# A fused attention, convolution and gated feed-forward kernel: the first feed-forward product split into three float16 products, the last batch in three query groups, a new order

## The chip, the cores and the metric

The kernel runs on one core of a Trainium2 chip. Its engines work side by side, each through its own list of instructions in order: TensorE (PE, with PEld for its weight loads), VectorE (DVE), ScalarE (ACT), GpSimd (POOL), and SyncE (SP), which issues every DMA here. They meet through semaphores. The metric is the device time of one execution in microseconds (us), lower is better. A profile gives the span from the first instruction to the last, which lies about 2 us under the time of the same execution.

## The reference

```python
def _attn_ref(q, k, v):                    # q, k, v: 4 batches x 8 heads x 1152 x 64, float32
    q_pool = q.reshape(B, H, S // 2, 2, D).mean(axis=3)          # 576 queries a head
    scores = (1 / np.sqrt(D)) * np.matmul(q_pool, k.transpose(0, 1, 3, 2))
    scores = scores - np.max(scores, axis=-1, keepdims=True)
    attn = np.exp(scores)
    attn = attn / (np.sum(attn, axis=-1, keepdims=True) + 1e-09)
    return np.matmul(attn, v)

def _moe_ref(x, w_in, conv_w, w_out):      # x: 4 x 576 x 512 (the heads side by side)
    h = np.maximum(x @ w_in, 0.0)          # 512 -> 1024, the "first product"
    hp = np.concatenate([zeros, h, zeros], axis=1)               # one token of padding at each end
    conv_out = sum(conv_w[k] * hp[:, k:k + S, :] for k in range(3))
    gate = 1.0 / (1.0 + np.exp(-conv_out))
    return h * gate @ w_out                # 1024 -> 512, the "second product"
```

The weights arrive as float64 words and are turned into float32 on the chip by bit operations (`weights`).

## The kernel before

Heads are worked in 16 pairs, four pairs to a batch. For each pair `loads` brings q, k and v, and brings v into float16 high and low parts, scaled by a power of two that is found from the largest sum of absolute values of a row (`abs_v`, `spread_v`, `top_v`, `pow_v`, `scale_v`, `hi_v`, `lo_v`).

`softmax(o, d)` handles one block of 128 queries of each head (d = 0 to 3; d = 4 holds the last 64 of both heads). PE makes the scores in float32 (L404), DVE takes the maximum of each row (L416), ACT the exponential with its sum (L421), DVE the inverse of the sum in two small instructions (L433, L437). For most heads the normalized block is written as a float16 high part (L460 on ACT or L455 on POOL) and a low part (DVE, L463), and both are transposed by DMA (L476). For the seven heads of `X32` it stays float32: it is normalized (L493) and PE transposes it (L506, taken out of PSUM at L511).

`values(o, y)` is the product with v for a query group y: 256 queries (d = 0, 1) or 320 (d = 2, 3, 4). It takes three float16 matmuls for each of nine blocks of keys (L535; for the `X32` heads one float32 matmul, L541). The two heads of a pair fill the two halves of the array's columns. ACT writes the result as float32 into `x` (L548).

`feed(b, u)` makes the first product for 255 or 321 tokens of a batch: for each of eight slices of 128 hidden columns four float32 matmuls over 257 or 323 columns (L575), which the trace shows as two passes each, so eight records in all. ACT applies the relu (L581); ACT or POOL makes the first tap (L585, L589), DVE the other two (L596), ACT the tanh (L602), DVE the gate (L606). `second(b, t)` makes the second product for one block of 128 tokens (L639; 64 tokens at t = 4, L645), ACT takes it out (L653), SP stores it.

The order of all work is fixed beforehand: every step is a task, the table ORDER says in which order the tasks are emitted, SLOTS which buffer of its ring each takes, and SWAPPED which tasks run on their other engine. Each engine runs its own tasks strictly in that order. For example a pair's low part is the task

```python
t = add("DVE", dve(S) - 0.025, low, after=[t], uses=[ps_[e], sm, hl], port=True)
```

The text below calls one block S: the second product of batch 2 for its tokens 256 to 383 (t = 2), eight matmuls of L639. It is the place from which the work left is PE's above all.

Of the kernel before, what the change touches and what calls it, by code (L numbers as in the profile page):

```python
# [8 lines left out]
F32 = mybir.dt.float32  # L9
# [54 lines left out]
class Plan:  # L64
# [23 lines left out]
def unpack(words):  # L88
# [29 lines left out]
pcCrpUCZpdpVpXqCCLp4p2Cspyp5qgCpqECIpYCMqdCJCtCSp6CKp7CBBXpZqeC0CNpiqaCuqhCCC1pWCvqbqip8qfCOqqqcpjCPCTC2qJqSCU
qrCQqKCVqsp9DdqLC3CWCwqjqtqnDkqTCXqoDequqyqMDfqNCDqUCYqvqpqkDgqVqODlqlqPq5qxC4qWDyqzqmqRqXqQC6rYq6qwCRq7tcqYq8
rWDzC7DrqZq9q2q0DFDmuADhDAC5raq3DGDsDnDtq4DBriC8C9DCrvDoDDq1DiDuqArbrwrfrjrxtdrZDaDprcDErgrlr1DHrdrhDbqBrmrkr2  # L120
DIDcrnreDqDvryDwroDjrpr3DxrIDLDJrqrsDZrzDMrrDNrJtfrKDOrttgrLDPrArurBr4rFDQuvrCD0rDrMsarGDRrEsdsbD1seDKDSr5rQsf
rNscr6rOr7rPD2sgqIshskrRsnsitir0sqsosjDTslspDUsrrHr9sssAuxD3sDstsmsBsxDVsEsCsyDWr8sFsNtethDXsGsQsHsOrSsusIszsK
sRsLsSDYEpsvsPsMtjsTtsrTs0sJttEqsXtks1tuEbtlswsYtvEcEduyEeEiErtwsUtxEfEDsVEgEjEss2EwsWtyEhtCs3tmEttFtnEEtDEkuu
ExtIsZEFs4tGEyEREltHEmuzEzD5tJESETD6tztos5s8tAtKs6tps7D7s9EuEntSEvtBtqEKtTtLtUtEEAtVtrELEGtPt5EMtWEBE5uwtMEHD4
EovNtQEID8EUE6ENtXEJEYD9tYE7EVEOuKt6tZEZE0EPEWtaEQt2tNECt7tOE8E1t3FcuBuLt4t0uMt8tbEXE9t1FduiE2t9FeuCvPFquDuauE
tRE3ubFaFfFjucFgFbFrudvQFxFhuFFsuGFkufFlFmFEFyujueugukuXFzFiFtFFuhuNulFnumFLuOunuPvMFSE4upFAFMuQFuuUuouYuRuqFN
uZuSFOvauTuruVFGuHu0FPvbFZuWu1vcF0FBu2uIuJFQvdFoFHvOFCFpvRvAFIu3FJveu4FvF1u7u5FTF2u8vfusFUvgu9vBvkF3FRvCFVFwF4
vlvnvTFWvmFKvqutFDFXFYvUF6GdvhvVvou6F5vrGevDvsviF7vEvpvjv5vFv2vWEaGfv3vHvtv6vxF8vuv7vGF9vyGav4vzv8wivXv9vvwfGb
wavwwcvIwgwjwhwdwswbwkvJwvwlwmGjwevYwnvZGkwtwpGcGlwov0wwGgwqwxwuv1GmwrGhwywzwFGnwAwIwCGovKwGwJwHwDwKw0wBwLwMwP
wEwSwNvSw1vLGvwTwUwOGJGwwVGxwWHbGKwXGXHcwQwYGyGCwZGYGLGMwRGQGDGEGFGzGpGAGZGqG0G1GNGrGOGPGsGBGRGSG4GtGTGuGUGGw2  # L130
G5Hiw3GHG2GVGWHpHjG6HkHdHeG3HwHfHqG7HgGIHrHhHlHmHKHxHsHtG8G9HYHLHyHMHzHaHAHRHBHZHCHDHSHTHUH0HNHnHVH5HoHWH1HuHX
HEHOIcH6H7HFH8H2IjHvH3HGIdIeHHHPIkIfHIH9IgIaHQIhIlIbH4IiHJImIqIpIxInIoIyIrIsIzIAItIBICGiIDIuIEIvIwIFIGIJIHIIIK
ILIMINIO
"""
SLOTS = (
    "00000010100011001001012110001020112111230321101030000011110011101011102001011120021102131022100031000201031111"
    "01112000002210221000012103110010000210201033011101011022210010001113011300100000110201101301110200013022101012"
    "03100111100000410100023011001110010101210223201013001011110231100200111521010121101111210020001320103200101112"
    "11101003101100000600002112200103011130021003221110013032210200111011120113100002112101011320303112121203111000"
    "02021002011100110112303211021302001031022000001113001120112011013002211010100031011122013011032000112000000111"  # L140
    "10112012100013012200231103011101123010001141210011222000201131031100123112003110100110000600112002203203110100"
    "12102331000123001010120011511112112302213200101010033211121112032301000001021020011002102112301002031102012211"
    "31301100110100002110032010121203011013312200121010000131200232210201012001311031232012103111204030001112001140"
    "10310204021100111101001001213011231304010210011020321411100100001110020140011033000203041001201042100312010110"
    "01010300211111431300110411211000221302140101111001"
)
SWAPPED = """
aeaobmb0dCeAeHfugcgqgGgZhjhxh5iiisiEiSjtjTkdkqkTk0lblLl8mbmimDm3ndnqntn5n8omoUo8pnqPrXsksxsUsXtftZuxuHuRu4vhvk
vuvxvEvZwmwpwMwPxcxlxVyNyWzezwzzz1AfAtAAAOCeCGCUC8ErEyEMETFeFlFNGxGEHdHkHFHTH7
"""  # L150

# [4 lines left out]
def tile_pooled_attention_conv_gate_ffn(  # L156
# [38 lines left out]
    wi = const.tile([P, KC, DFF], F32, name="wi")  # L195
    wo = const.tile([P, FC, DM], F32, name="wo")

# [4 lines left out]
    r_kt = Ring("kt", 3, sb, [P, S], F32)  # L202
    r_qt = Ring("qt", 2, sb, [P, K0], F32)
    r_qd = Ring("qd", 2, sb, [P, K1], F32)
    r_v = Ring("v", 2, sb, [P, 2, NC, P], F16)
# [4 lines left out]
    r_vs = Ring("vs", 3, sb, [P, 8], F32)  # L210
    r_x = Ring("x", 7, sb, [P, 578], F32)
    r_h = Ring("h", 5, sb, [P, 324], F32)
    r_g = Ring("g", 4, sb, [P, 4, 322], F32)
    r_o = Ring("o", 2, sb, [P, DM], F32)

    def pe(cycles):
        return cycles / 2400.0 + 0.1
# [6 lines left out]

    def gp(n):
        return 0.3 + n / 850.0


# [5 lines left out]
    for pr in range(NPAIR):  # L234
        o = Pair()
        o.pr, o.vin, o.qin = pr, Buf(r_vin), Buf(r_qin)
        o.kt, o.qt, o.qd = Buf(r_kt), Buf(r_qt), Buf(r_qd)

        o.x32 = [(pr, e) in X32 for e in range(2)]
        o.v, o.vs = Buf(r_v), Buf(r_vs)  # L240
        o.x = Buf(r_x)
        pairs.append(o)

    def loads(o):
# [54 lines left out]
        def abs_v():  # L299
            nc.scalar.activation(  # L300
                out=o.v[:, es].rearrange("p e c d -> p (e c d)")[:, 0:HS * len(two)],
                in_=o.vin[:, es].rearrange("p e c d -> p (e c d)"), func=AF.Abs, accum_out=o.vs[:, 0:1],
            )

        def spread_v():
            nc.tensor.matmul(
                out=wv[:, 0:P], lhsT=o.vs[:, 0:1].to_broadcast([P, P]), rhs=ident, start=True, stop=True
            )
# [530 lines left out]
```

## Time and profile before

| | |
|---|---|
| time, median of 3 runs | 652.01 us (650.74 to 653.11) |
| the profiled execution | 651.47 us, span 649.5 us |
| busy share of the span | PE 94%, DVE 82%, ACT 70%, POOL 24% |
| 16 DMA engines, hardware queue | 81.9% |
| granted TensorE clock, mean | 0.992 of 2.4 GHz |

A busy share is a mean over the whole span; stages differ, and a PE that counts as busy need not stream without a break. So the stages are read one by one from a table of windows, and what ended last is read from the chain of waits.

### The profile page before, as it was taken

How to read it: one execution, taken by the hardware profiler on the slowest of the kernel's cores; microseconds unless marked ns; L12 is line 12 of the kernel's file. 1: busy time of each engine (PE TensorE's matmuls, PEld its weight loads, DVE VectorE, ACT ScalarE, POOL GpSimd, SP SyncE). 2: the span in 40 equal slices, each digit the busy share in tenths (PEclk: the TensorE clock that was granted, in tenths of full speed). 3: DMA queues.
4: the chain of work that ended last, by engine and by line, in shares of the span. 5: the costliest groups of instructions: out<-in, count | busy, mean ns of one | idle time of the engine just before them, and what ended most of it. 6: DMA issues, size and time to landing. Idle time of an engine off the chain costs nothing. (4 is left out here: it accounts for less than half of the span.)

```text
span 649.5 us, 10435 instructions
## 1 busy us (share of the span) xinstructions
PE 612.6 (94%) x3805; PEld 380.1 (59%) x3805; DVE 535.5 (82%) x811; ACT 453.0 (70%) x775; POOL 158.7 (24%) x183
## 2 busy tenths in 40 slices
PE   4679898999999999999999999999999999999997
PEld 2355555666666655555666666455666655486643
DVE  4998999998899999788978899878988998764610
ACT  4998988787888776746678788757767765643410
POOL 0553334323231222221365000021231122220000
PEclk9998989899999999999999999999999999999999
DMA  8779988879875887999889998999998988983001
GB/s 279 190 207 196 215 227 168 187 150 228 178 179 122 171 201 139 229 203 209 167 221 179 233 154 204 197 180 215 191 220 167 172 191 162 192 134 58 0 22 67
DMA packets 279122, 113.72 MB, mean 175 GB/s; under 512 B 265376, under 2 KB 265888, under 8 KB 279072
## 3 DMA queue, kind: packets, MB, share of 16 engines
q1 hardware_dynamic: 279072, 113.07, 81.9%
q8 instruction: 30, 0.49, 0.3%
q14 instruction: 20, 0.16, 0.1%
HBM read 37.77 MB, written 4.72 MB: 65 GB/s over the span
## 5 line engine op out<-in xcount | busy, mean ns | idle before, releaser
L421 ACT ACTIVATE p<-s,sm 128x1152 f32<-128x1152 f32 x144 | 175.4, 1219 | 91.5 <-DVE sm L416 59.0
L416 DVE TENSOR_REDUCE sm<-s 128x1 f32<-128x1152 f32 x144 | 192.3, 1349 | 10.0 <-PE s L404 9.3
L404 PE MATMUL s<-kt,qt 64*128 64x512 f32 (+3 forms) x704 | 183.2, 471 | 17.2 <-ACT p L421 8.7
L463 DVE SCALAR_TENSOR_TENSOR hl<-p,sm,hl 128x1152 f16<-128x1152 f32 (+1 forms) x116 | 168.8, 1464 | 18.8 <-ACT hl L460 10.6
L404 PEld LDWEIGHTS s<-kt,qt 64*128 64x128 f32 (+1 forms) x704 | 89.1, 175 | 119.0 <-issue 81.9
L404 PE MATMUL s<-kt,qd 64*128 64x512 f32 x256 | 144.0, 647 | 0.0
L575 PE MATMUL a<-x,wi 128*128 128x257 f32 (+1 forms) x512 | 134.8, 414 | 0.6 <-ACT h L581 0.5
L535 PE MATMUL a<-pt,v 128*64 128x256 f16 (+1 forms) x1350 | 118.1, 288 | 0.1
L639 PE MATMUL a<-wo,g 128*128 128x512 f32 x256 | 115.1, 599 | 0.0
L575 PEld LDWEIGHTS a<-x,wi 128*128 128x128 f32 x512 | 93.8, 189 | 30.9 <-ACT h L581 1.9
L460 ACT ACTIVATE hl<-p,sm 128x1152 f16<-128x1152 f32 (+1 forms) x78 | 97.0, 1252 | 13.0 <-issue 3.9
L535 PEld LDWEIGHTS <-v 128*64 128x64 f16 x1350 | 87.8, 110 | 12.6 <-issue 4.4
L455 POOL TENSOR_SCALAR hl<-p,sm 128x1152 f16<-128x1152 f32 (+1 forms) x38 | 51.0, 1344 | 140.3 <-DVE sm L437 93.9
L639 PEld LDWEIGHTS a<-wo,g 128*128 128x128 f32 x256 | 47.1, 190 | 53.5 <-issue 51.4
L596 DVE SCALAR_TENSOR_TENSOR g<-h,cw,g 128x321 f32<-128x321 f32 (+1 forms) x128 | 65.1, 526 | 12.4 <-POOL g L589 8.5
L541 PE MATMUL a<-pt,v 128*64 128x256 f32 (+1 forms) x252 | 64.1, 409 | 0.5 <-ACT pt L511 0.5
L506 PE MATMUL a<-ident,p 128*128 128x128 f32 (+1 forms) x315 | 49.5, 280 | 14.0 <-ACT pt L511 6.4
L493 POOL TENSOR_SCALAR p<-p,sm 128x1152 f32<-128x1152 f32 (+1 forms) x27 | 37.6, 1394 | 87.6 <-DVE sm L437 68.4
L511 ACT ACTIVATE pt<-a 128x384 f32<-128x384 f32 (+2 forms) x98 | 45.0, 476 | 11.2 <-PE a L506 10.6
L506 PEld LDWEIGHTS a<-ident,p 128*128 128x128 f32 (+1 forms) x315 | 33.1, 143 | 27.6 <-ACT pt L511 8.9
L589 POOL TENSOR_SCALAR g<-h,cw 128x255 f32<-128x255 f32 (+1 forms) x24 | 17.4, 727 | 103.2 <-ACT h L581 92.8
L541 PEld LDWEIGHTS a<-pt,v 128*64 128x64 f32 x252 | 33.4, 137 | 11.1 <-ACT pt L511 1.0
(58 smaller groups left out, 467.6 us busy)
## 6 DMA issues: line engine op xcount, KB each, us to landing
qin<-in_q_dram SPq DMA_DIRECT2D x16, 640.0 KB, 5.2
kt<-in_k_dram SPq DMA_DIRECT2D x16, 576.0 KB, 4.9
vin<-in_v_dram SPq DMA_DIRECT2D x9, 576.0 KB, 4.7
g<-in_moe_w_in_dram SPq DMA_DIRECT2D x8, 512.0 KB, 5.0
qd<-qt SPq DMA_DIRECT2D x32, 128.0 KB, 4.1
g<-in_moe_w_out_dram SPq DMA_DIRECT2D x8, 512.0 KB, 4.3
out_dram<-o SPq DMA_DIRECT2D x16, 256.0 KB, 2.5
vin<-in_v_dram SPq DMA_DIRECT2D x7, 288.0 KB, 3.7
```

What stands on the lines that cost most here:

```text
L404: nc.tensor.matmul(out=w, lhsT=f, rhs=kk, start=True, stop=True)
L416: nc.vector.tensor_reduce(out=sm[:, e:e + 1], in_=runs(st[e]), axis=AX.XY, op=ALU.max, negate=True)
L421: nc.scalar.activation(out=p.tile().rearrange("p (a n) -> p a n", a=2), in_=runs(st[e]), func=AF.Exp, bias=sm[:, e:e + 1], scale=1.0, accu ...
L455: eng.tensor_scalar(out=hl[rows, 0], in0=ps_[e][rows], scalar1=sm[rows, 6 + e:7 + e], scalar2=1.0, op0=ALU.mult, op1=ALU.mult,)
L460: nc.scalar.activation(out=hl[rows, 0], in_=ps_[e][rows], func=AF.Copy, scale=sm[rows, 6 + e:7 + e])
L463: nc.vector.scalar_tensor_tensor(out=hl[rows, 1], in0=ps_[e][rows], scalar=sm[rows, 6 + e:7 + e], in1=hl[rows, 0], op0=ALU.mult, op1=ALU.s ...
L506: nc.tensor.transpose(w[:, (i - a1) * nq:(i - a1 + 1) * nq], ps_[e][rows, i * P:(i + 1) * P], ident[rows, rows])
L535: nc.tensor.matmul(out=to, lhsT=o.v[:, e, c, vc:vc + D], rhs=o.pt[y, e][:, hl * NC + c, 0:n], start=(c == 0 and j == 0), stop=(c == NC - 1 ...
L541: nc.tensor.matmul(out=to, lhsT=o.v[:, e, c].bitcast(F32), rhs=p32.rearrange("p (a n) -> p a n", a=NC)[:, c, 0:n], start=(c == 0), stop=(c ...
L575: nc.tensor.matmul(out=w[:, 0:n], lhsT=wi[:, j, f * P:(f + 1) * P], rhs=x.x[:, 255 * u:255 * u + n], start=(j == 0), stop=(j == KC - 1),)
L596: nc.vector.scalar_tensor_tensor(out=c, in0=h[:, t:t + tok], scalar=cw[:, f, t:t + 1], in1=c, op0=ALU.mult, op1=ALU.add)
L639: nc.tensor.matmul(out=w.tile(), lhsT=g[f // 4][:, f % 4, c:c + P], rhs=wo[:, f, :], start=(f == 0), stop=(f == FC - 1),)
```

## The change

Three things change together.

The first product is computed as three float16 matmuls in place of one float32 matmul (high times high, high times low, low times high). For that `w_in` is converted into the buffer of `w_out`, its row sums of absolute values are taken, and it is split into `wi` high and low (`split`); `w_out` is converted afterwards. The result of `values` goes to a new float32 buffer `xf`, and from there into `x` high (ACT or POOL) and `x` low (DVE). The scale of x for a batch comes from the v scales of its four pairs (`scales`), so the v scale is now found for the float32 heads too (`abs_one`, `most_v`). The relu undoes the scales.

The last batch has three query groups of 256, 256 and 64 queries, in `values` and `feed` alike (255, 256 and 65 tokens), and its pairs are worked interleaved, which the order table decides.

The order, the buffers and the engines of single tasks are searched anew, with one more buffer each for k, q and v. The small sum of the softmax (`total`) can run on ACT, normalizing a float32 head too, and the scaling steps of v move from POOL to DVE.

```diff
+GROUPS = [((0, 1), (2, 3, 4))] * 3 + [((0, 1), (2, 3), (4,))]
...
-    wi = const.tile([P, KC, DFF], F32, name="wi")
+    wi = const.tile([P, 2, KC, DFF], F16, name="wi")
...
-    r_kt = Ring("kt", 3, sb, [P, S], F32)
+    r_kt = Ring("kt", 4, sb, [P, S], F32)
...
-    r_x = Ring("x", 7, sb, [P, 578], F32)
+    r_xf = Ring("xf", 5, sb, [P, 320], F32)
+    r_x = Ring("x", 7, sb, [P, 2, 578], F16)
...
+        def abs_one():
+            m = HS * len(one)
+            nc.scalar.activation(
+                out=o.x.tile().rearrange("p a n -> p (a n)")[:, 1:1 + m] if m == HS else o.x[:, :, 1:1 + HS],
+                in_=o.v[:, of].bitcast(F32).rearrange("p e c d -> p e (c d)"), func=AF.Abs,
+                accum_out=o.vs[:, 6:7],
+            )
...
         def scale_v():
-            nc.gpsimd.tensor_scalar(
+            nc.vector.tensor_scalar(
...
-        iv = add("DVE", 0.265, inverse, after=ex, uses=[sm], port=True)
-        y = int(d > 1)
...
+        t = add("DVE", 0.13, total, after=ex, uses=[sm], port=True, alt=("ACT", 0.2, False))
+        iv = add("DVE", 0.135, inverse, after=[t], uses=[sm])
+        y = next(i for i, ds in enumerate(o.groups) if d in ds)
...
+        def high(eng):
+            if eng is nc.scalar:
+                nc.scalar.activation(out=o.x[:, 0, to], in_=xf[:, 0:n], func=AF.Copy, scale=o.bs[:, 2:3])
+                return
...
+        def low():
+            nc.vector.scalar_tensor_tensor(
+                out=o.x[:, 1, to], in0=xf[:, 0:n], scalar=o.bs[:, 2:3], in1=o.x[:, 0, to],
+                op0=ALU.mult, op1=ALU.subtract,
+            )
...
             def mm(f=f, w=w):
-                for j, x in enumerate(xs):
-                    nc.tensor.matmul(
-                        out=w[:, 0:n], lhsT=wi[:, j, f * P:(f + 1) * P], rhs=x.x[:, 255 * u:255 * u + n],
-                        start=(j == 0), stop=(j == KC - 1),
-                    )
+                for i, (a, c) in enumerate(((0, 0), (0, 1), (1, 0))):
+                    for j, x in enumerate(xs):
+                        nc.tensor.matmul(
+                            out=w[:, 0:n], lhsT=wi[:, a, j, f * P:(f + 1) * P], rhs=x.x[:, c, s0:s0 + n],
+                            start=(i == 0 and j == 0), stop=(i == 2 and j == KC - 1),
+                        )
...
             def relu(w=w, h=h):
-                nc.scalar.activation(out=h[:, 0:n], in_=w[:, 0:n], func=AF.Relu)
+                nc.scalar.activation(out=h[:, 0:n], in_=w[:, 0:n], func=AF.Relu, scale=xs[0].bs[:, 3:4])
...
+            def total():
+                _, lo32, hi32, mm, a = parts()
+                i = KC * c + j
+                nc.scalar.activation(out=mm, in_=a, func=AF.Abs, accum_out=ws[:, i:i + 1])
...
+                def low(src=src, to=to):
+                    nc.vector.scalar_tensor_tensor(
+                        out=wi[:, 1, to[0], to[1]], in0=src, scalar=ws[:, 12:13], in1=wi[:, 0, to[0], to[1]],
+                        op0=ALU.mult, op1=ALU.subtract,
+                    )
```

What the new order does is shown at three places by the instruction lists of single engines (name of the tile written, arrow, tiles read; `x3` counts equal neighbours). The first is DVE where the first feed-forward block begins, before (`g` holds the taps, the rows with `g<-g 128x512` and `wo` convert weights):

```order
L463 SCALAR_TENSOR_TENSOR hl<-p,sm,hl 64x1152
L705 TENSOR_SCALAR g<-g 128x512
L416 TENSOR_REDUCE sm<-s 128x1
L596 SCALAR_TENSOR_TENSOR g<-h,cw,g 128x255
L714 TENSOR_SCALAR wo<-g 128x512
L596 SCALAR_TENSOR_TENSOR g<-h,cw,g 128x255 x2
```

And DVE at the same place of the changed kernel:

```order
L609 SCALAR_TENSOR_TENSOR x<-xf,bs,x 128x320
L501 SCALAR_TENSOR_TENSOR hl<-p,sm,hl 128x1152
L446 TENSOR_REDUCE sm<-s 128x1
L609 SCALAR_TENSOR_TENSOR x<-xf,bs,x 128x320
L474 RECIPROCAL sm<-sm 128x2
L322 TENSOR_SCALAR vs<-vs 128x1
L446 TENSOR_REDUCE sm<-s 128x1
L501 SCALAR_TENSOR_TENSOR hl<-p,sm,hl 128x1152
L799 TENSOR_SCALAR g<-g 128x512
L689 SCALAR_TENSOR_TENSOR g<-h,cw,g 128x255
```

New there are the low parts of x (L609) between the softmax steps, while the sum before a reciprocal (L433 before) is gone from some places. In all, 239 DVE instructions stand ahead of the first tap, 243 before.

The second place is ACT at the start of the program, before:

```order
L421 ACTIVATE p,sm<-s,sm 128x1152 x2
L460 ACTIVATE hl<-p,sm 128x1152
L300 ACTIVATE v,vs<-vin 128x576
L421 ACTIVATE p,sm<-s,sm 128x1152
L701 ACTIVATE g<-g 128x512
L511 ACTIVATE pt<-a 128x3x128
```

And changed (L851 takes the absolute sums of `w_in`, L464 is the softmax's `total`, L532 normalizes a float32 head):

```order
L451 ACTIVATE p,sm<-s,sm 128x1152
L851 ACTIVATE g,ws<-wo 128x512
L451 ACTIVATE p,sm<-s,sm 128x1152
L289 ACTIVATE qt<-qin 128x640
L498 ACTIVATE hl<-p,sm 128x1152
...
L464 ACTIVATE sm<-sm 128x2
L451 ACTIVATE p,sm<-s,sm 128x1152
L532 ACTIVATE p<-p,sm 128x1152
```

ACT has taken in work between the exponentials: 196 instructions stand ahead of its first relu, 157 before.

The third place is the end of PE's list, before:

```order
L535 MATMUL a<-pt,v 64x320
L575 MATMUL a<-x,wi 128x257 x4
L575 MATMUL a<-x,wi 128x323 x32
L639 MATMUL a<-wo,g 128x512 x32
L645 MATMUL a<-wo,g 64x256 x16
```

And changed:

```order
L733 MATMUL a<-wo,g 128x512 x4
L668 LDWEIGHTS wi
L668 MATMUL a<-x,wi 128x67
...
L733 MATMUL a<-wo,g 128x512 x18
L739 MATMUL a<-wo,g_6567 64x256 x8
L739 MATMUL a<-wo,g_6628 64x256 x8
```

Before, all five blocks of the last second product stood behind the last first product; now 14 of the 32 matmuls of the four large blocks stand between the short 67-column groups.

## Rows read from the trace of the kernel before

**Rows 1.** The page, part 1: busy us (share of the span), instructions

```profile
PE 612.6 (94%) x3805; PEld 380.1 (59%) x3805; DVE 535.5 (82%) x811; ACT 453.0 (70%) x775; POOL 158.7 (24%) x183
```

**Rows 2.** Table of windows: stretch, length, busy us by engine (instructions), clock, DMA share

```profile
core 0: us, PE busy (x) PEld busy (x) DVE busy (x) ACT busy (x) POOL busy (x), PEclk, DMA share, GB/s
8.00:139.00 131.00, 111.62 (x751) 69.07 (x752) 121.99 (x191) 112.15 (x192) 48.54 (x47) 0.96 0.86 205
139.00:248.00 109.00, 106.79 (x696) 71.28 (x695) 102.33 (x162) 86.17 (x159) 30.43 (x38) 1.00 0.81 179
248.00:533.00 285.00, 282.52 (x1784) 172.76 (x1783) 250.10 (x364) 207.83 (x341) 62.31 (x72) 1.00 0.96 191
533.00:649.50 116.50, 111.59 (x582) 66.87 (x580) 59.33 (x93) 44.19 (x82) 16.71 (x22) 1.00 0.47 95
```

**Rows 3.** Timeline of PE where block S begins: start, us, instruction

```profile
532.95 1.02 PE L639 MATMUL a<-wo,g 128*128 128x512 f32 x2
```

**Rows 4.** Waits of DVE from 8 to 248: us in total, times, longest

```profile
DVE sm L433 <- ACT p L421: 4.7, 7, 1.4
DVE sm L416 <- PE s L404: 3.5, 8, 0.7
```

**Rows 5.** Pieces of the chain that ended last: start us, us, what, records

```profile
566.70 6.74 PE a L535 x108
...
574.66 8.88 PE a L575 x40
...
591.17 3.79 PE a L535 x54
594.96 19.37 PE a L575 x72
```

**Rows 6.** Timeline of PE, transposes of 64 columns after a load of 128

```profile
110.93 0.28 PE L506 MATMUL a<-ident,p 64*128 64x64 f32 x2
...
111.05 0.60 PE L506 MATMUL a<-ident,p 64*128 64x64 f32 x7
```

**Rows 7.** Groups of DVE by shape: busy us, mean ns, idle before

```profile
L463 DVE SCALAR_TENSOR_TENSOR hl<-p,sm,hl 128x1152 f16<-128x1152 f32 x109 | 157.9, 1456 | 18.6 <-ACT hl L460 10.6 <-POOL hl L455 6.1 <-POOL x L358 1.4
...
L596 DVE SCALAR_TENSOR_TENSOR g<-h,cw,g 128x321 f32<-128x321 f32 x64 | 34.4, 553 | 7.2 <-POOL g L589 5.5 <-ACT g L585 1.3
L596 DVE SCALAR_TENSOR_TENSOR g<-h,cw,g 128x255 f32<-128x255 f32 x64 | 31.1, 499 | 5.2 <-POOL g L589 3.0 <-ACT g L585 1.9
...
L352 DVE SCALAR_TENSOR_TENSOR v<-vin,vs,v 128x576 f16<-128x576 f32 x25 | 20.8, 846 | 2.4 <-POOL v L344 2.0 <-POOL x L358 0.4
...
L278 DVE TENSOR_TENSOR qin<-qin 128x640 f32<-128x640 f32 x9 | 7.4, 817 | 3.5 <-DMA qin<-in_q_dram 3.5
...
L493 DVE TENSOR_SCALAR p<-p,sm 128x1152 f32<-128x1152 f32 x7 | 5.7, 815 | 0.0
```

**Rows 8.** Pieces of DVE in the same chain: start us, us, what

```profile
547.30 0.17 DVE sm L433
...
547.58 0.06 DVE vs L321
...
584.57 0.89 DVE g L596 x2
```

**Rows 9.** Groups of ACT by shape: busy us, mean ns, idle before

```profile
L460 ACT ACTIVATE hl<-p,sm 128x1152 f16<-128x1152 f32 x73 | 90.8, 1252 | 11.6 <-ACT p L421 3.1 <-DVE sm L437 3.0 <-issue 2.6
...
L421 ACT ACTIVATION_READ_ACCUMULATOR p<-s,sm 128x1 f32 x144 | 28.3, 197 | 0.0
...
L548 ACT ACTIVATE x<-a,vs 128x256 f32<-128x256 f32 x16 | 7.5, 468 | 4.8 <-POOL x L358 3.1 <-PE a L535 1.5 <-PE a L541 0.2
```

**Rows 10.** Windows of the same table, two dense stretches

```profile
20.00:120.00 100.00, 84.03 (x574) 52.02 (x574) 94.59 (x154) 89.01 (x152) 39.03 (x39) 0.95 0.87 200
180.00:260.00 80.00, 78.72 (x467) 49.54 (x463) 76.79 (x116) 62.06 (x111) 19.26 (x25) 1.00 0.76 158
```

**Rows 11.** Timeline of PE where the first product begins

```profile
139.36 1.35 PE L575 MATMUL a<-x,wi 128*128 128x257 f32 x5
```

More of the change, by code (lines that the diff above doesn't have):

```diff
@@ L525, in values @@
     def values(o, y):
-        n = (256, 320)[y]
+        first = P * o.groups[y][0]
+        n = min(P * (o.groups[y][-1] + 1), HS) - first
         w = Buf(r_a)
@@ L545, in part @@
                             )
+        xf = Buf(r_xf)
+        to = slice(1 + first, 1 + first + n)
         def keep():
             nc.scalar.activation(
-                out=o.x[:, 1 + 256 * y:1 + 256 * y + n], in_=w[:, 0:n], func=AF.Copy,
-                scale=1.0 if all(o.x32) else o.vs[:, 4:5],
-            )
-        t = None
-        for i in range(1):
-            t = add("PE", (n * 27.0 / 2400 * (4 / 3 if any(o.x32) else 1) + 0.08), lambda i=i: part(i), mode=2,
-                    after=o.turned[y] + o.vls + ([t] if t else []),
-                    uses=[o.v, o.pt[y, 0], o.pt[y, 1]] + ([w] if i else []), takes=[] if i else [w])
@@ new lines, in low @@
+        def low():
+            nc.vector.scalar_tensor_tensor(
+                out=o.x[:, 1, to], in0=xf[:, 0:n], scalar=o.bs[:, 2:3], in1=o.x[:, 0, to],
+                op0=ALU.mult, op1=ALU.subtract,
+            )
+        t = add("PE", (max(n, 90) * 27.0 / 2400 * (4 / 3 if any(o.x32) else 1) + 0.08), lambda: part(0), mode=2,
+                after=o.turned[y] + o.vls, uses=[o.v, o.pt[y, 0], o.pt[y, 1]], takes=[w])
+        t = add("ACT", act(n, 0.1), keep, after=[t] + o.one, uses=[w] + ([] if all(o.x32) else [o.vs]), takes=[xf])
@@ L563, in feed @@
     def feed(b, u):
-        tok = TOK[u]
+        xs = pairs[b * NP:(b + 1) * NP]
+        groups = xs[0].groups
+        s0 = P * groups[u][0] - 1 if u else 0
+        tok = (HS if u == len(groups) - 1 else P * (groups[u][-1] + 1) - 1) - s0
         n = tok + 2
-        xs = pairs[b * NP:(b + 1) * NP]
         need = [x.xs[y] for x in xs for y in range(u + 1)]
-        gs = [Buf(r_g) for _ in range(2)]
+        gs = [Buf(r_g if u < 2 else r_g2) for _ in range(2)]
         done = []
@@ L751, in weights @@
                 alt=("DVE", dve(m) - 0.05, True))
-        ready.append(t)
-    gated = []
-    for o in pairs:
-        o.pt, o.turned, o.xs = {}, [[], []], []
-        loads(o)
-        for d in range(5):
-            softmax(o, d)
-        for y in range(2):
-            values(o, y)
+        if src is w_in:
+            def total():
+                _, lo32, hi32, mm, a = parts()
+                i = KC * c + j
+                nc.scalar.activation(out=mm, in_=a, func=AF.Abs, accum_out=ws[:, i:i + 1])
+            t = add("ACT", act(m, 0.2), total, after=[t], uses=[tmp])
@@ L762, in tile_pooled_attention_conv_gate_ffn @@
+    gated = []
     for c in range(2):
         for j in range(KC):
+            plan.tag = ('weights', 0, j, c)
             weights(w_in, j, c, wi_ready[c])
+    plan.tag = ('split', )
+    split()
+    plan.tag = ('weights', 1)
     weights(conv_w, 0, 0, cw_ready)
     for j in range(FC):
+        plan.tag = ('weights', 2, j)
         weights(w_out, j, 0, wo_ready)
+    for o in pairs:
+        o.pt, o.xs = {}, []
+        o.turned = [[] for _ in o.groups]
+        plan.tag = ('loads', o.pr)
+        loads(o)
+        if o.pr % NP == NP - 1:
+            plan.tag = ('scales', o.pr)
+            scales(o.pr // NP)
@@ L768, in tile_pooled_attention_conv_gate_ffn @@
+    for o in pairs:
+        for d in range(5):
+            plan.tag = ('softmax', o.pr, d)
+            softmax(o, d)
+        for y in range(len(o.groups)):
+            plan.tag = ('values', o.pr, y)
+            values(o, y)
     for b in range(B):
-        gs, done = zip(feed(b, 0), feed(b, 1))
+        plan.tag = ('feed', b)
+        gs, done = zip(*[feed(b, u) for u in range(len(pairs[b * NP].groups))])
         for t in range(5):
+            plan.tag = ('second', b, t)
             second(b, gs, done, t)
```

304 lines of the change are left out of this document (208 added, 96 removed).

## The prediction

> **What bounds the kernel now.** The page first: PE is busy for 94% of the span, DVE for 82%, ACT for 70% [rows 1]. Read by stage these shares change places [rows 2]. From 8 to 139 us DVE is busy 122.0 of 131 us and PE 111.6, so DVE paces and PE starves; ACT with 112.2 is close behind. From 139 to 248 both are dense, PE 98%, DVE 94%. From 248 to 533 PE is busy 99% and DVE 88%. Behind block S, which begins at 532.95 [rows 3], PE has 111.6 us of work in 116.5 and DVE only 59.3: there PE alone sets the end, which the chain of waits shows too: its last pieces are PE's, L535 and L575 one behind the other, 19.37 us in one of them [rows 5]. DVE's own waits up to 248 us are small: 4.7 us for the exponential, 3.5 for scores [rows 4]. So up to 248 us DVE is about as full as the order allows, and then PE takes over.
>
> The change takes work from PE and gives some to DVE and ACT. The sum has to ask both.
>
> **PE.** In the chain, 40 passes of 257 columns take 8.88 us, 0.222 each [rows 5]; 72 passes, eight of them of 257 columns and 64 of 323, take 19.37, so one of 323 takes 0.275. A slice (eight passes) costs 1.78 and 2.20 us. A float16 pass over 128 weight columns is not in the trace. The nearest row is L535: 54 matmuls of 320 columns, two side by side, take 3.79 us [rows 5], 27 pairs of 0.140 or 0.44 ns a column, and the piece of 108 has the same rate (6.74 us). At 0.44 a pass of 257 or 258 columns is 0.113, one of 323 is 0.142, and a slice of twelve costs 1.36 and 1.70. For 67 columns the load of 128 weight columns may set the pace. The nearest rows are transposes that each load 128 columns and stream 64: two take 0.28 us, seven 0.60, so 0.064 for each one more [rows 6]. Bounds: 67 x 0.44 = 0.029 below, a 257-column pass, 0.113, above. I take 0.064.
>
> Batches 0 to 2: 3 x 8 x (1.78 + 2.20 - 1.36 - 1.70) = 22.1 us saved. Batch 3: 8 x (1.78 + 2.20) = 31.8 becomes 8 x 2 x 1.36 + 96 x 0.064 = 27.9, 3.9 saved (7.2 at the lower bound, a loss of 0.8 at the upper). `values` of the last batch turns four blocks of 320 columns (3.79 each) into four of 256 (6.74 - 3.79 = 2.95) and four of 64 (27 pairs at 0.064, 1.73): 3.6 us more (0.3 less at 0.028 a pair, 8.8 more at 0.113). Net 22.4 us less, so PE is busy about 590. All of it is on the path only where PE paces.
>
> Here a rule of the Trainium skill speaks against the short group. The transposes with 128 loaded columns start 0.064 us apart [rows 6]. "TensorE: Matmul & The Clock Gate", section "LDWEIGHTS (loading the stationary operand)", has a load take its columns over 1.2 in ns, which I estimate at 0.107 us for 128. By that the 96 short matmuls cost 4.1 us more than in the sum. The row disagrees, for a float32 load, and I keep to the row.
>
> **DVE.** A record's mean holds a tail in which the next instruction already runs: two taps in a row take 0.89 us [rows 8] at a mean of 0.499 [rows 7], so one occupies 0.39. I take 0.11 off each mean. Low parts of x: 20 of 256 columns at 0.39, 12 of 320 at 0.44, 4 of 64 at 0.235 (the slope between the two tap rows) make 14.0. Scalars per partition (the two scaling steps moved from POOL, the batch scales, the maxima): some 64 at the 0.06 of L321 [rows 8], with two short reductions 4.3. The sums in front of the reciprocal: 49 of 80 leave for ACT at 0.17 [rows 8], -8.3. Low parts of the weights: four of 1024, between 0.846 at 576 and 1.456 at 1152 [rows 7], 1.21 each, 4.8. The last batch's extra taps and gates (16 x (0.235 - 0.05), and little for gates) 3.2. Two more sums of q at 0.817, two more normalizations at 0.815 [rows 7], one weight addition less (some 0.6): 2.2. Together 20.2 us, DVE 556. Counted in program order, 2.2 of them lie behind S (low parts of x and the short taps there, less two row maxima and two low parts of v), so ahead of S there are 474.4 [rows 2] + 18.0 = 492.4 us. Where small instructions cost their full means of some 0.14 in place of 0.06, this is 5 us more; where the sums were paid as waits anyway, it is no less.
>
> **ACT, POOL, SP.** ACT gains some 40 us: nine normalizations at 1.25 [rows 9], 49 sums at about 0.2 as for an accumulator read, 27 high parts at about 0.47, eight sums over weights at 0.9, seven over v, three weight splits, less ten high parts of the softmax. It ends near 494, 77% of the span. POOL stays near 155. SP issues the same transfers. Their 16 engines are 96% busy from 248 to 533 [rows 2], which only an earlier S would tighten; over 8 to S the share rises by some two points, and no wait of PE for a transposed block is a large row now. They lie beside the rest.
>
> **The sum.** S can't begin before DVE has done its 492.4 us. Behind it PE has 116.5 us now; 3.9 are saved and 3.6 added, so about 116. With a DVE share s from 8 to S the time is 8 + 492.4 / s + 116 + 2, the 2 being what the profiled execution takes beside its span (651.47 against 649.5). I make the sum against 651.5; the median is 0.5 higher. At s = 0.937 nothing is gained. From 8 to 248, where DVE paced, s was 224.3 / 240 = 0.935. Two long stretches did better: 94.6% from 20 to 120, 96.0% from 180 to 260, the latter with PE at 98% [rows 10]. From 248 to 533 s was 0.88 because PE paced, and that is the part the removed passes open. One more buffer each for k, q and v lets loads come earlier, and half of the sums now follow their exponential on ACT itself, which is the longest wait in [rows 4]. I take 0.95: 8 + 518.3 + 116 + 2 = 644.3, **645 us**. PE alone would allow less: 651.5 - 22.4 = 629.
>
> The new hop of `values` (high part, then low part in DVE's queue) costs nothing where other blocks stand between on PE, as those of the next pair do. With that cover gone it is an ACT and a DVE instruction, about 0.9 us a group, 8 us for nine groups.
>
> **Rivals.**
> *DVE runs better than it ever did for long*, at 0.965 to 0.98, and the time comes to 629 to 637, where PE's own sum lies. For it: PE's new slack. Against: 0.96 is the best stretch of 80 us [rows 10]. Chance 0.12.
>
> *Forecast*: s from 0.945 to 0.96, 639 to 648. Chance 0.43.
>
> *No change*: s stays at 0.934 to 0.94, as where DVE paced before; what PE saves turns into its waits for DVE. 650 to 653.5. For it: the share of 0.935 over 240 us. Against: the eased waits. Chance 0.20.
>
> *Slower: ACT paces the front.* Ahead of its first relu ACT has 20 us more (the weight sums, splits, v sums, softmax sums; 196 instructions for 157), on top of 112 us. At DVE's 93% this takes until 8 + 132 / 0.93 = 150 in place of 139.4 [rows 11]. DVE then has done what it had by 139, about 124 us, and keeps 368 of its 492; at 0.95 S begins at 538 and the end is 656. It decides from a first relu later than 147. For it: ACT at 86% in that stage [rows 2] and a strict order. Against: DVE has no more to do ahead of the first tap than before, so some of the delay is shared. The same happens at 0.93 or less for any other reason. 654 to 668, chance 0.22.
>
> *Loads set the pace of the short groups*, up to 0.113 a matmul, where two loads could not overlap: 96 x 0.049 = 4.7 us behind S, and the forecast becomes 650. The skill's rule above gives 0.107 and 649. [Rows 6] speak against it. Chance 0.03.
>
> **How the numbers follow.** A measurement of this kernel tells about 0.3% from no change (650 to 653.5 on this base). The last rival falls to the three in equal parts. Faster: 0.12 + 0.43 + 0.01, 0.56. Same: 0.20 + 0.01, 0.21. Slower: 0.22 + 0.01, 0.23. The range reaches from inside the first rival, 632, to the middle of the slower one, 659; outside lie about 0.06 below and 0.12 above. The likeliest case alone is 639 to 649.
>
> **What would show it.** Right: float16 passes of 257 columns start 0.11 us apart, of 67 about 0.06; PE busy near 590, DVE near 556; DVE 94 to 96% from 8 to S; S near 527, and 116 us behind it; no stage in which PE is 99% busy while DVE is under 90%, save behind S. Wrong: first relu later than 147 with ACT over 92% before it; DVE waiting for ACT (sums, high parts of x) more than the 5 us of now up to 248; short matmuls at 0.1 apart; PE waiting behind S.

## The result and the profile after

The changed kernel takes 647.02 us (median of 14 runs, 644.53 to 649.71), the kernel before 652.07 beside it (14 runs). The ratio is 0.9916, 95% interval 0.9893 to 0.9938: about 5 us faster, by more than a measurement is uncertain. The profiled execution took 645.35 us, with a span of 643.6.

First the page, part 1, of the changed kernel, against [rows 1].

```profile
PE 597.1 (93%) x4375; PEld 370.6 (58%) x4375; DVE 559.7 (87%) x894; ACT 491.4 (76%) x905; POOL 153.4 (24%) x167
```

PE has lost 15.5 us, DVE has gained 24.2 and ACT 38.4. The table of windows, over the same stretches as [rows 2]:

```profile
core 0: us, PE busy (x) PEld busy (x) DVE busy (x) ACT busy (x) POOL busy (x), PEclk, DMA share, GB/s
8.00:139.00 131.00, 108.09 (x659) 66.24 (x658) 123.15 (x197) 116.34 (x219) 44.87 (x41) 0.91 0.86 206
139.00:248.00 109.00, 104.47 (x776) 68.46 (x772) 106.55 (x162) 97.24 (x186) 28.31 (x30) 1.00 0.86 174
248.00:533.00 285.00, 277.94 (x2039) 169.87 (x2038) 268.95 (x419) 222.28 (x385) 65.30 (x66) 1.00 1.00 193
533.00:643.60 110.60, 105.96 (x907) 65.56 (x905) 60.19 (x117) 53.44 (x115) 14.20 (x26) 1.00 0.51 101
```

From 248 to 533 us DVE has risen from 88% to 94.4% and PE fallen from 99% to 97.5%. The timeline of PE shows block S and the start of the first product, against [rows 3] and [rows 11].

```profile
153.63 1.49 PE L668 MATMUL a<-x,wi 128*128 128x257 f16 x12
...
532.07 1.98 PE L733 MATMUL a<-wo,g 128*128 128x512 f32 x4
```

The first product begins 14 us later than before. S begins at 532.1, in place of 532.95: ahead of S only 0.9 us was gained. Behind it lie 643.6 - 532.1 = 111.5 us, in place of 116.5. So 5 of the 6 us in the span came from behind S. In the seven runs of the changed kernel below whose edits lie ahead of S or in the transfers, the same 111.5 us (to 0.1) lie behind it. Two runs whose edits lie wholly behind S began it at 531.2 and 533.6, so the place of S varies by 1 to 2 us from one execution to the next. The 0.9 us ahead of S are no more than that; the 5.0 behind it are as much as the medians differ by. There the chain of waits (against [rows 5]) shows the short groups:

```profile
588.40 1.73 PE a L739 x16
590.12 0.85 PE a L580 x54
590.98 9.50 PE a L668 x84
...
607.46 0.39 PE a L668 x12
607.85 1.80 PE a L733 x4
...
620.30 15.53 PE a L733 x36
635.83 3.63 PE a L739 x32
```

Twelve passes of 67 columns take 0.39 us, 0.033 each; 27 pairs of `values` over 64 columns take 0.85, 0.031 a pair; 84 passes of 258 columns take 9.50, 0.113 each. Of DVE's waits from 8 to 248 us ([rows 4]) these are the two longest:

```profile
DVE g L799 <- ACT g L795: 3.5, 2, 2.5
DVE sm L446 <- PE s L434: 3.1, 6, 0.8
```

The wait for the exponential's sum has fallen to 1.7. Of DVE's groups by shape ([rows 7, 8] have those of before), those that the prediction costed and that are read below:

```profile
L609 DVE SCALAR_TENSOR_TENSOR x<-xf,bs,x 128x256 f16<-128x256 f32 x20 | 9.5, 479 | 1.9 <-ACT x L602 1.9
...
L609 DVE SCALAR_TENSOR_TENSOR x<-xf,bs,x 128x320 f16<-128x320 f32 x12 | 6.6, 547 | 0.0
L908 DVE SCALAR_TENSOR_TENSOR wi<-wo,ws,wi 128x1024 f16<-128x1024 f32 x4 | 5.0, 1274 | 0.0
...
L352 DVE TENSOR_SCALAR vs<-vs 128x1 f32<-128x1 f32 x16 | 2.4, 149 | 0.2
...
L609 DVE SCALAR_TENSOR_TENSOR x<-xf,bs,x 128x64 f16<-128x64 f32 x4 | 1.2, 303 | 0.8 <-ACT x L602 0.8
L627 DVE TENSOR_SCALAR bs<-vs 128x1 f32<-128x1 f32 x4 | 1.1, 266 | 0.0
```

### The profile page after: what moved, and what is told of

It reads as the page before. It is cut to its first block, busy times and chain, and to the rows that moved or that the text cites. A ratio compares the mean times of both kernels' runs of the same rounds, so it can differ in the third digit from the quotient of the medians.

```text
span 643.6 us, 11730 instructions
## 1 busy us (share of the span) xinstructions
PE 597.1 (93%) x4375; PEld 370.6 (58%) x4375; DVE 559.7 (87%) x894; ACT 491.4 (76%) x905; POOL 153.4 (24%) x167
## 4 chain that ended last, share of the span: by engine, by line
PE 34%; DVE 10%; issue 5%; ACT 4%; POOL 1%; ACTq 0%; DVEq 0%; POOLq 0%
PE a L733 12%; PE a L668 8%; PE s L434 7%; PE a L580 5%; DVE hl L501 4%; DVE sm L446 3%; ACT p L451 2%; DVE g L689 1%; PE a L739 1%; POOL hl L493 1%; DVE g L699 1%; PE a L586 1%; DVE v L374 0%; ACT hl L498 0%; PE a L550 0%
## 5 line engine op out<-in xcount | busy, mean ns | idle before, releaser
L434 PE MATMUL s<-kt,qt 64*128 64x512 f32 (+3 forms) x704 | 196.1, 487 | 21.1 <-ACT p L451 13.1
L493 POOL TENSOR_SCALAR hl<-p,sm 128x1152 f16<-128x1152 f32 (+1 forms) x48 | 64.0, 1334 | 256.8 <-DVE sm L474 177.8
L580 PE MATMUL a<-pt,v 128*64 128x256 f16 (+2 forms) x1566 | 119.5, 272 | 0.0
L668 PE MATMUL a<-x,wi 128*128 128x257 f16 (+3 forms) x864 | 104.5, 274 | 1.6 <-ACT o L747 0.9
L668 PEld LDWEIGHTS <-wi 128*128 128x128 f16 x864 | 76.8, 98 | 29.6 <-issue 10.7
L498 ACT ACTIVATE hl<-p,sm 128x1152 f16<-128x1152 f32 (+1 forms) x68 | 84.5, 1250 | 11.6 <-DVE sm L474 7.8
L689 DVE SCALAR_TENSOR_TENSOR g<-h,cw,g 128x255 f32<-128x255 f32 (+3 forms) x144 | 70.9, 508 | 14.9 <-ACT g L678 10.7
L674 ACT ACTIVATE h<-a,bs 128x257 f32<-128x257 f32 (+3 forms) x72 | 33.7, 471 | 20.8 <-PE a L668 16.6
L682 POOL TENSOR_SCALAR g<-h,cw 128x255 f32<-128x255 f32 (+3 forms) x31 | 24.0, 776 | 76.2 <-ACT h L674 63.1
L434 PEld LDWEIGHTS s<-kt,qd 64*128 64x128 f32 x256 | 40.0, 195 | 2.0 <-DMA qd<-qt 2.0
```

The source lines that it names most:

```text
L434: nc.tensor.matmul(out=w, lhsT=f, rhs=kk, start=True, stop=True)
L493: eng.tensor_scalar(out=hl[rows, 0], in0=ps_[e][rows], scalar1=sm[rows, 6 + e:7 + e], scalar2=1.0, op0=ALU.mult, op1=ALU.mult,)
L498: nc.scalar.activation(out=hl[rows, 0], in_=ps_[e][rows], func=AF.Copy, scale=sm[rows, 6 + e:7 + e])
L580: nc.tensor.matmul(out=to, lhsT=o.v[:, e, c, vc:vc + D], rhs=o.pt[y, e][:, hl * NC + c, 0:n], start=(c == 0 and j == 0), stop=(c == NC - 1 ...
L668: nc.tensor.matmul(out=w[:, 0:n], lhsT=wi[:, a, j, f * P:(f + 1) * P], rhs=x.x[:, c, s0:s0 + n], start=(i == 0 and j == 0), stop=(i == 2 a ...
L689: nc.vector.scalar_tensor_tensor(out=c, in0=h[:, t:t + tok], scalar=cw[:, f, t:t + 1], in1=c, op0=ALU.mult, op1=ALU.add)
```

## The experiments

The theory on trial is the prediction's: ahead of S the time is DVE's work over a share of 0.95. Its rivals are that PE still sets the pace there, that transfers or ACT do, or that several do at once. Each run is compared with the changed kernel (647.02 us, S at 532.1) or with the kernel before (S at 533.0); the kernel before, measured beside each group, moved by no more than 1.5 us. S is the start of the same matmul in the timeline of PE each time, read from the one profiled execution.

**PE relieved ahead of S.** Two of the three products in batches 0 to 2:

```diff
-                for i, (a, c) in enumerate(((0, 0), (0, 1), (1, 0))):
+                many = ((0, 0), (0, 1)) if b < 3 else ((0, 0), (0, 1), (1, 0))
+                for i, (a, c) in enumerate(many):
...
```

> The changed kernel with two of the three float16 products in the first product of batches 0 to 2 (w_in low times x high is left out there), so 24 slices lose four passes of 257 and four of 323 columns: 24 x 4 x (0.110 + 0.139) = 23.9 us of PE, all ahead of block S. If DVE sets the pace ahead of S (95.0% busy from 8 to 533), the time falls by 0 to 4 us, to 643 to 647, and S begins at 528 to 532. If PE still sets it there (97.5% busy from 248 to 533), most of the 24 us comes back: 623 to 630, S at 508 to 515.

Measured: 643.74 us (ratio to the kernel before 0.9856, 0.9824 to 0.9887), S at 530.9. 24 us less of PE moved S by 1.2 (3.3 in the medians). PE did not set the pace alone.

**DVE relieved ahead of S.**

```diff
 def tap(t, f=f, h=h, g=g):
-                c = g[:, f % 4, 0:tok]
+                w = 16 if b < 3 else tok
+                c = g[:, f % 4, 0:w]
...
-                    out=c, in0=h[:, t:t + tok], scalar=cw[:, f, t:t + 1], in1=c, op0=ALU.mult, op1=ALU.add
+                    out=c, in0=h[:, t:t + w], scalar=cw[:, f, t:t + 1], in1=c, op0=ALU.mult, op1=ALU.add
```

> The changed kernel with the two DVE taps of batches 0 to 2 made over 16 columns in place of 255 or 321 (the rest of those columns keeps the first tap alone): 96 instructions fall from 0.39 or 0.44 us to some 0.12, 48 x (0.27 + 0.32) = 28 us of DVE, all ahead of S. If DVE sets the pace ahead of S, the time falls by 18 to 26 us (PE, with 33 us of slack up to S, stops it there), to 621 to 629. If PE sets it, by under 4: 643 to 647.

Measured: 643.53 us (0.9863, 0.9821 to 0.9904), S at 529.2. DVE was busy 24.2 us less in all (535.5 for 559.7), and S moved by 2.9 (3.5 in the medians). So the theory falls as it was stated: by the prediction's own formula S had to come 25 us earlier. The tables of windows of the two cuts, PE's first, from 248 to 533 us:

```profile
248.00:533.00 285.00, 267.23 (x1904) 157.46 (x1903) 270.20 (x418) 222.63 (x386) 64.31 (x68) 0.99 1.00 193
```

```profile
248.00:533.00 285.00, 280.56 (x2081) 172.39 (x2079) 252.37 (x421) 223.64 (x388) 64.60 (x70) 1.00 1.01 196
```

With PE cut, DVE stays at 94.8% and PE falls to 93.8%. With DVE cut, PE goes to 98.4% and DVE to 88.6%. The engine whose work was left alone stays as full as it was, and the relieved one idles. But the DMA share is 1.00 and 1.01 in both, so transfers could have been the reason as well.

**Both cuts together.** The two diffs above in one kernel:

> Both cuts of the runs before together: batches 0 to 2 with two products in place of three (24 us of PE) and with their two DVE taps over 16 columns (28 us of DVE). Alone each moved S by 1.2 and 2.9 us only. Theory of a shared pace (PE and DVE are both nearly full ahead of S and each covers for the other): together S comes 15 to 24 us earlier, 623 to 632. Rival, transfers pace (the DMA engines are 100% busy from 248 to 533 in the changed kernel and stay so in both cuts) or ACT does: 638 to 643, as with one cut alone.

Measured: 630.97 us (0.9651, 0.9629 to 0.9672), S at 517.3: 14.8 us earlier, where the single cuts gave 1.2 and 2.9 (16 us in the medians, for 3.3 and 3.5). PE and DVE hold the stretch together. This came with the DMA share at 1.03 (248 to 515 us):

```profile
248.00:515.00 267.00, 256.77 (x1873) 152.72 (x1873) 242.35 (x397) 214.19 (x373) 57.74 (x62) 1.00 1.03 201
```

**Transfers relieved**, on top of both cuts and alone. The transposes bring the high parts only, and `values` reads them twice:

```diff
-                        out=pt[:, :, c:c + rows.stop - rows.start],
-                        in_=hl[rows].rearrange("p a n -> p (a n)"),
+                        out=pt[:, 0:NC, c:c + rows.stop - rows.start],
+                        in_=hl[rows, 0],
...
-                                out=to, lhsT=o.v[:, e, c, vc:vc + D], rhs=o.pt[y, e][:, hl * NC + c, 0:n],
+                                out=to, lhsT=o.v[:, e, c, vc:vc + D], rhs=o.pt[y, e][:, c, 0:n],
```

> The same two cuts, and the DMA transposes bring the high parts alone (half the bytes of each; values reads the high part in place of the low part too, with as many matmuls). If transfers pace, this is what frees them: 12 us or more under the kernel with the two cuts alone. If PE and DVE pace together, within 5 us of it.

> The changed kernel with nothing cut but the transposes, which bring the high parts alone (values reads the high part twice). If transfers set the pace ahead of S: S at 522 or earlier and 637 or less. If PE and DVE do, as they stand at 97.5% and 94.4% from 248 to 533: 644 to 647.

Measured: 633.74 us with both cuts (S at 521.1, later than without the third cut), and 644.61 alone (0.9859, 0.9834 to 0.9885; S at 532.4). The windows of the one that was cut alone:

```profile
248.00:515.00 267.00, 260.58 (x1939) 160.44 (x1937) 251.10 (x387) 207.53 (x361) 62.47 (x62) 1.00 0.61 127
```

The share of the 16 engines fell from 1.00 to 0.61 and S did not move. Transfers do not pace this stretch, full as they look: none of the 10 us and more came that were expected if they did. The median is 2.4 us under the changed kernel's, about as much as either single cut gave; the profiled execution, the slowest of the four, does not show where that comes from. Nor does a trace here show why the same cut cost 2.8 us with both others in place.

**ACT relieved**, on top of both cuts:

```diff
-                c = g[:, f % 4, 0:tok]
+                c = g[:, f % 4, 0:16 if b < 3 else tok]
                 nc.scalar.activation(out=c, in_=c, func=AF.Tanh, scale=0.5)
...
-                in_=o.vin[:, es].rearrange("p e c d -> p (e c d)"), func=AF.Abs, accum_out=o.vs[:, 0:1],
+                in_=o.vin[:, es].rearrange("p e c d -> p (e c d)")[:, 0:64], func=AF.Abs, accum_out=o.vs[:, 0:1],
...
```

> The same two cuts, and ACT relieved of some 28 us ahead of S: the tanh of batches 0 to 2 over 16 columns (48 x 0.24 = 11 us), the absolute sums of v over 64 columns (13.5) and those of the first product's weights over 64 (3). If ACT paces once PE and DVE are free: 10 us or more under the kernel with the two cuts alone. If not, within 4 us of it.

Measured: 630.46 us, S at 516.6. ACT had 21 us less from 8 to 515 (408.7 for 430.1), and 0.5 us came of it. ACT relieved alone, without the two cuts, was not tried. What sets the pace once PE and DVE are both relieved (PE at 96% and DVE at 91% from 248 to 515 us) was not found.

**The old price of the product in the new order.**

```diff
+                many = ((0, 0), (0, 1), (1, 0)) + ((1, 1),) * (b < 3)
...
```

> The changed kernel with a fourth float16 product (low times low) in the first product of batches 0 to 2: 24 slices gain four passes of 257 and four of 323 columns, 23.9 us of PE ahead of S. A slice then costs 16 x 0.110 = 1.76 and 16 x 0.139 = 2.22 us, the price of the float32 product before (1.78 and 2.20), so this is the new order without the cheaper product. If PE and DVE share the pace ahead of S, PE now binds alone: its 490 + 24 us at the 98 to 99% that it reaches give S at 545 to 552, 660 to 667, slower than the kernel before. If the new order itself made the gain: 647 to 651.

Measured: 665.11 us (1.0186, 1.0151 to 1.0222), S at 551.9. With the product at its old price the rest of the change costs 18.9 us ahead of S (551.9 for 533.0), and the cheaper product gives back 19.8. Its windows, and its longest wait of DVE from 8 to 533 (7.1 us for the same in the changed kernel), show PE full and DVE waiting for it:

```profile
248.00:533.00 285.00, 281.63 (x2109) 176.47 (x2108) 256.40 (x392) 212.32 (x370) 60.98 (x64) 1.00 0.95 185
```

```profile
DVE sm L446 <- PE s L434: 17.0, 23, 1.9
```

**The same cuts in the old order.** Three of the four float32 matmuls of a slice, in all batches, and in a second kernel the narrow taps too:

```diff
-                for j, x in enumerate(xs):
+                for j, x in enumerate(xs[0:3]):
...
```

> The kernel before with three of the four float32 matmuls of a first-product slice (the fourth pair of heads is left out), in the old order and with no work added on DVE or ACT: 24 x (0.445 + 0.55) = 23.9 us less PE ahead of S, 8.0 behind. If PE held DVE back from 248 us to S (PE 99%, DVE 88%), both stretches give it back: 651.5 - 8 - 18 to 24 = 620 to 626. If the order itself holds both engines, only the part behind S comes: 640 to 644.

> The kernel before with three of the four float32 matmuls of a first-product slice (24 us less PE ahead of S, 8 behind) and the two DVE taps of batches 0 to 2 over 16 columns (28 us less DVE). PE's cut alone brought S forward by 5.3 us and the time to 644. If the old order too is paced by both engines at once: S at 513 to 520, 629 to 636. If other ties of the old order (DVE's waits of 12 us for the exponential's sum and 10 for high parts, from 139 to 533) hold it: S at 524 or later, 640 to 644.

Measured: 643.96 us (0.9875, 0.984 to 0.9909; S at 527.7) and 634.34 (0.9716, 0.9683 to 0.9748; S at 519.1). Had PE held DVE back in the old order, where DVE was busy only 88% of the time from 248 to S, 24 us less of PE would have been worth 18 to 24. They were worth 5.3; 8.6 more came when DVE was cut too. The window of the first kernel, against [rows 2]:

```profile
248.00:533.00 285.00, 273.43 (x1730) 162.75 (x1728) 253.08 (x369) 208.00 (x342) 63.41 (x75) 1.00 0.97 194
```

DVE's share rose from 0.88 to 0.89 only. Its 12% of idle time was no reserve that PE's relief could open. What DVE's cut alone would have done in this order was not tried. Behind S, 8 us less of PE gave back 2.8 (641.5 - 527.7 = 113.8, for 116.5).

**PE behind S, less and more.** Less: the product left out above, in batch 3 alone (`if b == 3`). More: the short group over 257 columns.

```diff
+                k, m = (s0 - 190, 190) if u == 2 else (s0, 0)
...
-                            out=w[:, 0:n], lhsT=wi[:, a, j, f * P:(f + 1) * P], rhs=x.x[:, c, s0:s0 + n],
+                            out=w[:, 0:m + n], lhsT=wi[:, a, j, f * P:(f + 1) * P], rhs=x.x[:, c, k:k + m + n],
...
```

> The same product left out in batch 3 alone: 16 slices lose four passes of 257 or 258 columns and 8 lose four of 67, 8 x 4 x (0.110 + 0.112 + 0.032) = 8.1 us of PE, behind S. If PE alone sets the end behind S, the time falls by 6.5 to 8, to 639 to 640.5. If the chain ACT, DVE, PE of the last groups sets it, by under 3.

> The changed kernel with the first product of the last batch's short group computed over 257 columns in place of 67 (the 190 others are thrown away): 96 passes of 0.110 in place of 0.032 us, 7.5 us of PE more, all behind S. This is the upper bound that the prediction put on a 67-column pass (0.113). If PE alone sets the end behind S: 7 to 7.5 us more, 654. If the groups' chain over ACT and DVE sets it there: under 3 us more, 647 to 650.

Measured: 641.85 us (0.9843, 0.9807 to 0.9879) with less, 653.83 (1.0011, 0.9988 to 1.0034) with more. Behind S the first has 639.3 - 531.2 = 108.1 us, the second 651.5 - 533.6 = 117.9. So 7.5 us more of PE cost 6.4, nearly all; 8.1 us less gave back 3.4 there (5.2 in the medians), between the two cases that were expected. The chain of the kernel with less, and PE's two longest waits in it from 530 us on, show why:

```profile
588.74 4.58 PE a L669 x40
593.32 0.17 SPq L514
593.53 4.76 DMA pt<-hl
598.34 1.04 PE a L580 x54
```

```profile
PE a L580 <- DMA pt<-hl: 1.3, 2, 1.1
PE a L669 <- ACT h L675: 1.3, 3, 0.8
```

PE now arrives before the last transposes have landed and before ACT has emptied a result, and a DMA stands in the chain where matmuls of the first product stood. All its waits there come to 4.4 us, for 0.3 in the changed kernel, so about half of what PE saved turned into waiting.

**Work taken off DVE by other engines.** Two products in all batches, no low parts of the weights, all sums of q on POOL, all softmax sums on ACT:

```diff
-                for i, (a, c) in enumerate(((0, 0), (0, 1), (1, 0))):
+                for i, (a, c) in enumerate(((0, 0), (0, 1))):
...
-            t.engine = t.alt[0]
+            if t.fn.__name__ != "sum_q":
+                t.engine = t.alt[0]
+        for t in self.tasks:
+            if t.fn.__name__ == "total" and t.alt:
+                t.engine = "ACT"
```

> Two of the three products in all four batches (w_in low times x high and the low parts of the weights are left out), and DVE relieved by 19 us without losing more of the computation: the 11 sums of q that run on DVE go to POOL (9.0 us), the 31 softmax sums to ACT (4.8, at 0.2 each there 6 more), the weights' low parts are gone (5.0). PE loses 24 us ahead of S and 8.1 behind. If PE and DVE share the pace ahead of S, both are freed: S 8 to 13 us earlier, and with the 5 us measured behind S 628 to 634. If only one of them counts, or POOL's longer sums (1.5 us for 0.8) hold up the loads: 637 to 642.

Measured: 649.62 us (0.9944, 0.9924 to 0.9965), S at 539.7, a miss. PE and DVE both have less to do than in the changed kernel, and S comes 7.6 us later. DVE's and PE's longest waits from 8 to 533 us:

```profile
DVE sm L478 <- ACT sm L468: 14.6, 18, 2.1
```

```profile
PE s L438 <- ACT p L455: 30.9, 42, 2.4
```

The same two came to 1.6 and 13.1 us in the changed kernel. A softmax sum on ACT stands in ACT's strict list behind whatever is ahead of it, and DVE, whose reciprocal is the next in its own list, stops until it is done. Which share of the loss belongs to the sums of q on POOL (1.67 us each there) was not separated.

## Why the prediction came out right, and which of its steps did not

The time (645 forecast) and the sign were right; the reason was only half right. S came 5 us later than the 527 of the forecast, and what lies behind it took 4.5 us less than the 116. The two misses cancel, so that the time came out this close is in good part luck.

*The sum.* s from 8 to S was forecast at 0.95. Measured: (123.15 + 106.55 + 268.95) / 525 = 0.950. But the step "S can't begin before DVE has done its 492.4 us" took DVE as the pace and PE as a looser bound at 629. The runs show a common pace: either engine relieved by 24 us alone brings 1 to 3 us, both together 15, and 24 us more on PE cost 20. The reason given for the share, "From 248 to 533 s was 0.88 because PE paced, and that is the part the removed passes open", does not hold in the old order, where 24 us less of PE left it at 0.89. In the new order it holds in part: the share is 0.90 with four products, 0.944 with three and 0.948 with two. So 0.95 is what DVE reaches beside a PE at 97.5% in this order, and not a property of DVE. Had the change cut more from one engine, the formula would have failed, as it does for the narrow taps by 22 us. All these cuts lie behind the start of the first product; which engine paces the front, up to 153 us, was not tried by relieving one alone.

*DVE's work* was 498.65 us ahead of S, 6.3 over the forecast, 559.7 in all for 556. Two terms were too small. One the prediction named, with its bound of 5 us: instructions on one value per partition, taken at 0.06, have records of 0.14 to 0.27 us here. The other is the low parts of x, taken at their means less 0.11: they are busy for 9.5 + 6.6 + 1.2 = 17.3 us, nearly their number times their means, for 14.0. By the sum S then falls at 8 + 498.65 / 0.95 = 532.9, in place of 527; it began at 532.1. That does not show that the extra work delayed it: work and share are read from the same 525 us, so the quotient gives their end whatever paces. By the narrow taps, 24.2 us of DVE's work alone are worth 2.9.

*Behind S* 116 us were forecast and 111.5 measured. The mis-sized term is the short group: 0.064 a pass, taken from float32 transposes [rows 6], where the chain shows 0.033 and 0.031. 96 x 0.031 + 4 x 27 x 0.033 = 6.5 us, against a miss of 4.5. So the 5 us of the result lie where the prediction had put next to none, and of the 6 us that it had put ahead of S 0.9 came, no more than S varies by.

*PE.* The longer passes were right: 0.113 us for 258 columns, as forecast. PE's busy time was forecast at 590 and is 597.1, though the short groups were cheaper. The first stage has a granted clock of 0.91 for 0.96 in [rows 2], and the records of the scores' 512 columns have a mean of 672 ns for 647. How the excess splits between the two was not settled.

*The slower rival.* Its condition was met: the first relu began at 155.2 us, later than its 147 and its 150. Its price was not due. The table of windows, from 8 us to just behind that relu:

```profile
8.00:157.00 149.00, 125.34 (x793) 77.60 (x792) 140.95 (x226) 132.31 (x251) 50.33 (x47) 0.92 0.86 203
```

The step that failed is "DVE then has done what it had by 139, about 124 us": DVE had done 141 us by then, busy for 94.6%. It needs the first relu only where its own list reaches the first tap, which began here before and after:

```profile
173.42 0.47 DVE L596 SCALAR_TENSOR_TENSOR g<-h,cw,g 128x255 f32<-128x255 f32 x1
...
166.37 0.48 DVE L689 SCALAR_TENSOR_TENSOR g<-h,cw,g 128x255 f32<-128x255 f32 x1
```

Before, the tap stood 31 us behind the first relu (142.0 us), with other work between; now it stands 11 us behind. So the relu came 13 us later and the tap 7 us earlier, with 239 instructions ahead of it for 243, and from the relu to the tap DVE waited for no relu. The prediction's own word against this rival, "DVE has no more to do ahead of the first tap than before", was right. What delayed the first product was not tried. ACT stood at 89%, under the 92% named as a sign, and PE itself was busy for longer ahead of it, at a lower clock, before and after:

```profile
8.00:139.30 131.30, 111.92 (x752) 69.19 (x752) 122.29 (x191) 112.45 (x193) 48.84 (x47) 0.96 0.86 205
...
8.00:153.60 145.60, 122.06 (x764) 74.87 (x762) 137.55 (x222) 130.31 (x248) 48.43 (x45) 0.92 0.85 202
```

*The other rivals.* A DVE share of 0.965 or more did not come, nor one of 0.94. That loads pace the short groups at up to 0.113 is refuted by 0.033. Here the rule that the prediction weighed, from the Trainium skill, "TensorE: Matmul & The Clock Gate", section "LDWEIGHTS (loading the stationary operand)", gave an estimate of 0.107 for 128 columns; as the spacing of passes the trace does not agree, nor with my own 0.064. The same page of the Trainium skill, section "Weight-path perf modes — Fast Weight Load (FWL) and DoubleRow", says that a load of 128 columns that is not float32 is faster, about twice as measured there; this points the way of the trace, whose records of such loads have a mean of 98 ns in float16 and of 190 in float32.

## What to carry to other kernels

Where two engines are both at about 90% or more in a stretch, take from one in thought and ask whether the other has room: a sum over either one alone mistakes a share for a reserve, and a cut pays when both get it. Where each engine runs a fixed list, a small step moved to an idler engine can cost more than it saves, since it waits there behind that engine's own work (seen in one run here, which moved two kinds of step at once). And a result that comes late holds an engine up only from the place where that engine's list first needs it: DVE had other work for 31 us behind the first relu, and a relu that came 13 us later did not delay its first tap.

## What was not expected of the hardware

A float16 pass of 67 columns with a load of 128 weight columns in front starts 33 ns after the one before it, under a third of a pass of 257 (110 to 113 ns), so short groups were almost free of a fixed cost here.

The 16 DMA engines show a share of 1.00 to 1.04 from 248 us on, and S still came 14.8 us earlier when PE and DVE were relieved; to halve the transposes brought it no earlier. The Trainium skill, "Perfetto Trace Analysis", section "Identifying the Most-Contended Engine", calls the occupancy of the 16 engines misleading, and the runs agree. The same section of the Trainium skill tells the reader to optimize the engine with the highest occupancy first (TensorE it judges by other measures); for DVE at 95% that was worth 2.9 us out of 24.

The granted clock fell in the front of the changed kernel. The page, part 2, rows of PE and of the clock in slices of 16.1 us:

```profile
PE   4769887799999999999999999999999999999997
...
PEclk9899996699999999999999999999999999999999
```

In the seventh and eighth slice, 97 to 129 us, it was 0.6 of 2.4 GHz, so PE spent part of them at the lower level of 1.2; PE is busy for seven tenths there, and for eight tenths in the two slices ahead. DVE was busy for 94% from 100 to 139 us all the same; what the lower clock cost was not measured.
